# Products of no use behind each flag product, behind the list counts and ahead of the first turned rows of the first routing

## The chip, the cores and the metric

The kernel runs on one core of one Trainium2 chip. The metric is the device time of one execution in microseconds (us), the median of several runs. TensorE is called PE, VectorE DVE, ScalarE ACT, GpSimd POOL and SyncE SP.

## What is computed

Three layers follow each other. A gated linear attention over 768 steps makes 3072 rows of 320 numbers. A mixture of eight experts gives each row to one expert, 384 rows to each, in the order of all gate logits; the rows of an expert then go through that expert's two matrices. A dense layer with an exponential unit ends it.

```python
def _moe_ref(x, w_gate, w1, w2):
    logits = x @ w_gate
    order = np.argsort(-logits.flatten())
    for idx in order:                       # greedy, largest logit first
        tok, e = (int(idx) // E, int(idx) % E)
        if assigned[tok] >= 0 or counts[e] >= cap:
            continue
        assigned[tok] = e
        counts[e] += 1
    for e in range(E):
        mask = assigned == e
        h = np.maximum(x[mask] @ w1[e], 0.0)
        out[mask] = h @ w2[e]

def _moe2_ref(x, w_in, w_out):
    h = x @ w_in
    g = np.where(h > 0.0, h, np.exp(np.minimum(h, 0.0)) - 1.0)
    return g @ w_out
```

## The kernel before, in words

The attention runs first, in 24 units. Then comes the routing, in eight rounds: each round finds the one expert whose list fills next, and the 384 rows of that list. The first round must be done before any expert work can start; rounds 1 to 7 are recorded in between the matmuls of the expert and dense layers (the class `Mlp`). Each engine works through its own list of instructions in the order in which they were recorded.

**The first round** (`Router.round` with `r == 0`) looks for a threshold on the logits in six steps, some bits at a time. A step after the first is a circle of two engines:

- DVE subtracts the last digit (`j`, L831; `d`, L834) and builds a table of comparisons (`ge`, L630).
- PE counts with it, in 12 small matmuls into `pr` (L802; the first step has 24 at L817).
- DVE compares the counts with what each expert can still take and writes flags (`half` L669, `flag` L670; `fl` L820 in the first step).
- PE sums the flags over the partitions in one matmul of 8 columns (L828, **the flag product**), and DVE reduces its result to the next `j`.

In between, one piece of the conversion of the last weight matrix (`wout_pieces`) is recorded in each step. It uses DVE (`wt`, L967 and L974), POOL (the product `wt<-wt,wx` at L977 and the subtraction `wol` at L1082) and ACT.

After the sixth step DVE finds the expert (`m`) and the rows of its first weights (`wi`, L845). POOL gathers the expert's first matrix with `wi` (`stg`, L1104). PE makes **the list counts**, three matmuls (`p1`, L863 to L865). DVE numbers the members of the list with them, and PE turns the numbers into row indices in 24 small matmuls (L889). DVE adds these up to `idx`, and POOL gathers with it the 384 rows in three pieces (`xg`), and behind them the expert's second matrix (`stg<-in_w2a`).

**The first turned rows** are made in `prep_x(0)`: for each of the three pieces PE transposes (L1176), ACT and DVE split the result into two parts (`xh` L1193, `xl` L1184). Then PE starts on the expert's first product (P1, `ph` at L1223) and goes on with the second (C1, `acc` at L1315 and after).

**Products of no use.** `spin(n)` (L1158) records n matmuls of 512 columns with the dense layer's weights `wih`, whose result `junk` nobody reads. `prep_x(0)` has them ahead of each piece's transposes and behind the last: `WARM = [8, 2, 2, 2]`. `junk` is one of the three PSUM buffers `acc`. The attention has such a row too, at its start (L145).

Of the kernel before, what the change touches and what calls it, by code (L numbers as in the profile page):

```python
# [8 lines left out]
F32 = mybir.dt.float32  # L9
# [21 lines left out]
SPIN, MX = 12, [256, 512, 640]  # L31
TG = 20
NB, NL, PX = 2, 3, 0.2
WARM = [8, 2, 2, 2]


class Plan:
# [50 lines left out]
    def next(self):  # L88
        self.due(min(self.todo)[0])
# [462 lines left out]
class Router:  # L552
# [180 lines left out]
    def round(self, r):  # L733
# [21 lines left out]
        if last:  # L755
            te = self.T([128, 8], F32, "te")
            V.scalar_tensor_tensor(te, neg, 0.0, self.w8, op0=ALU.is_equal, op1=ALU.mult)
            plan.dve(170)
        else:
            steps = STEPS[r > 0]  # L760
            if r > 0:
                Lm = self.T([128, 8, 24], F32, "Lm")
                V.scalar_tensor_tensor(Lm, neg[:, :, None].to_broadcast([128, 8, 24]), 3e38, L, op0=ALU.mult, op1=ALU.add)
                V.scalar_tensor_tensor(rem, neg, -3e38, rem, op0=ALU.mult, op1=ALU.max)
                V.tensor_reduce(b, Lm.rearrange("p i c -> p c i"), AX, ALU.max)
                yield plan.dve(1130) - HOP, "d", 0
                dg = self.digits(r)
                next(dg)
                V.tensor_tensor(self.cols(Lm), self.cols(Lm), self.over(b, 8), op=ALU.is_equal)
                next(dg)  # L770
                V.tensor_tensor(self.cols(Lm), self.cols(Lm), self.values(1, 8), op=ALU.mult)
                next(dg, 0)
                d = self.T([128, 24, 2], BF, "d")
                V.tensor_copy(d, self.D[:, 0, :, None].to_broadcast([128, 24, 2]))
                V.tensor_reduce(a8, Lm.rearrange("p i c -> p c i"), AX, ALU.max)
                yield plan.dve(2370) - HOP, "d", 0
                V.scalar_tensor_tensor(a8, ax, 0.0, a8, op0=ALU.is_equal, op1=ALU.mult)
                self.low_digits(r)
                plan.dve(1320)
                V.tensor_tensor(self.cols(A), self.values(1, 8), self.over(a8, 8), op=ALU.is_equal)  # L780
                plan.dve(350)
            for i in range(len(steps)):
                end = i == len(steps) - 1
                if i or r:
                    ge = self.pairs(d, ALU.is_ge)
                    self.table = self.made
                    t = plan.dve(600)
                    if i == 1 and r == 0:
                        self.low_digits(r)
                    if end:  # L790
                        d1 = self.T([128, 24], F32, "d1")
                        V.tensor_scalar(d1, d[:, :, 0], 1.0, None, op0=ALU.add)
                    else:
                        h = self.T([128, 24], F32, "h")
                        V.scalar_tensor_tensor(h, d[:, :, 0], 64.0, self.Df[:, i + 1], op0=ALU.mult, op1=ALU.add)
                    plan.dve(176)
                    yield t, "", 400
                    pk = self.psum()
                    fl = self.flag[i % 2]
                    if r == 0:  # L800
                        for g in range(12):
                            PE.matmul(pk[:64, :16].rearrange("p (i b) -> p i b", b=2), ge[:, g * 64:g * 64 + 64],  # L802
                                      A[:, :, g * 2:g * 2 + 2], start=g == 0, stop=g == 11)
                        yield plan.small(320), "d", 0
                        self.halves(pk[:64, :16].rearrange("p (i b) -> p b i", b=2), rem, fl[:32])
                    for g in range(6 if r else 0):
                        PE.matmul(pk[:, :32].rearrange("p (i b) -> p i b", b=4), ge[:, g * 128:g * 128 + 128],  # L807
                                  A[:, :, g * 4:g * 4 + 4], start=g == 0, stop=g == 5)
                    if r:
                        yield plan.small(160), "d", 0  # L810
                        self.fold(pk[:, :32].rearrange("p (i b) -> p b i", b=4), rem, fl[:32], ALU.is_ge)
                    t = plan.dve(793 if r else 320)
                else:
                    fl = self.T([128, 8], BF, "fl")
                    pk = self.psum()
                    for c in range(24):
                        PE.matmul(pk[:, :8], self.g0[:, c], A[:, :, c], start=c == 0, stop=c == 23)  # L817
                    yield plan.small(624), "d", 0
                    next(self.dg)
                    V.tensor_tensor(fl, pk[:, :8], rem, op=ALU.is_ge)  # L820
                    for _ in self.dg:
                        pass
                    h = self.T([128, 24], F32, "h")
                    V.scalar_tensor_tensor(h, self.Df[:, 0], 64.0, self.Df[:, 1], op0=ALU.mult, op1=ALU.add)
                    t = plan.dve(540)
                yield t, "", 400 if i else 0
                pn = self.psum()[:, :8]
                PE.matmul(pn, self.ones if end else self.onz, fl, start=True, stop=True)  # L828
                yield plan.small(39), "d", 0
                j = self.T([128, 1], F32, "j")  # L830
                V.tensor_reduce(j, pn, AX, ALU.max)  # L831
                if not end:
                    d = self.T([128, 24, 2], BF, "d")
                    V.tensor_scalar(d, h[:, :, None].to_broadcast([128, 24, 2]), j, None, op0=ALU.subtract)  # L834
                    plan.dve(440)
            te = self.T([128, 8], F32, "te")
            V.scalar_tensor_tensor(te, pn, j, self.w8, op0=ALU.is_equal, op1=ALU.mult)
# [25 lines left out]
        PE.matmul(p1[:, :48], self.ones, mm, start=True, stop=True)  # L863
        PE.matmul(p1[:, 48:], self.tri, mm, start=True, stop=False)
        PE.matmul(p1[:, 48:], self.far, mm, start=False, stop=True)  # L865
        yield plan.small(90), "d", 0
        inc = self.T([128, 48], F32, "inc")
        iv = self.T([128, 24], I32, "iv")
# [40 lines left out]
class Mlp:  # L909
# [255 lines left out]
    def prep_x(self, r):  # L1165
# [6 lines left out]
        def turn(k):  # L1172
            for t in range(3):
                if (r, t) == (0, 0):
                    self.twice(k, 0)
                nc.tensor.transpose(ps[k][0][:, t * 128:t * 128 + 128], self.xg[k][:, t * 128:t * 128 + 128], self.ident)  # L1176
# [20 lines left out]
        if r == 0:  # L1197
            ps = [self.psum() for t in range(3)]
            for k in range(3):
                self.spin(WARM[k])  # L1200
                turn(k)
                split(k)
            self.spin(WARM[3])
            return
# [283 lines left out]
    def start(self, first):  # L1488

        nc = self.nc  # L1490
        fill = self.fill
        self.ws = {}
        early = []
        need = "d"
        for k, (_, _, gap) in enumerate(first):
            if gap and k > FK:
                self.after(self.router.table)
                while True:
                    d = "d" in need
                    _, need = next(fill)  # L1500
                    if d and "d" in need:
                        break
            if not early and 0 in self.router.res:
                for i in range(3):
                    self.get_w(0, i)
                early = [q for i in range(3) for q in self.pieces(i)]
        self.routed = 0
        self.get_x(0)
        self.after()
        for h, l, x, p in early:  # L1510
            nc.scalar.activation(h, x, AF.Copy)
        for k, (h, l, x, p) in enumerate(early):
            nc.vector.tensor_tensor(l[p], x[p], h[p], op=ALU.subtract)
            if k % 2 and k < 4:
                self.get_w(0, 3 + k // 2)
        self.wsplit = 3
        routes = self.routes(1)
        for _ in range(R1):
            next(routes)
        plan = self.plan  # L1520
        plan.reset()
        self.junk = self.acc.tile([128, 512], F32, name="acc")
        for _ in self.prep_x(0):
            pass
        return fill, routes
# [137 lines left out]
```

## Time and profile before

| | before |
|---|---|
| median of 3 runs | 754.86 us (754.59 to 755.6) |
| the profiled execution's own time | 750.71 us |
| its span, first to last instruction | 748.9 us |
| its mean granted TensorE clock | 0.969 of 2.4 GHz |
| PE busy | 702.9 us (94%) |

The profiled execution is 4.15 us shorter than the median of the runs. Everything read from the trace is on the profile's own clock; what a change adds or takes away there is added to the median.

### The profile page before, as it was taken

The page shows a single profiled execution, that of the slowest core. Times are in us where ns is not written, and L with a number is a line of the kernel's source. Part 1 is how long each engine was busy: PE and PEld are TensorE (multiplying, and loading weights), DVE is VectorE, ACT ScalarE, POOL GpSimd, SP SyncE. Part 2 cuts the span into 40 slices and gives each one's busy share as a digit, 9 for nine tenths or more (in the row PEclk, how much of TensorE's full clock was granted, in tenths as well). Part 3 has the DMA queues.
Part 4 walks back from the last instruction along what each step waited for, and adds up shares of the span by engine and source line. Part 5 has one row for each costly group of instructions (what it writes and reads, how often), then busy time and mean ns, then how long its engine had stood idle before and what let it go on. Part 6 is the DMA issues. An engine that isn't in the chain of part 4 may idle for free.

```text
span 748.9 us, 17930 instructions
## 1 busy us (share of the span) xinstructions
PE 702.9 (94%) x7274; PEld 639.3 (85%) x7274; DVE 541.3 (72%) x1592; ACT 377.6 (50%) x804; POOL 186.6 (25%) x242
## 2 busy tenths in 40 slices
PE   7889888837999999999999999999999999999997
PEld 4656666626989999999999999999999999999997
DVE  8687888887898968965896698569868833851442
ACT  5455445435365725842772366256527743752443
POOL 5666655235111401210301120112022220001001
PEclk9899999957999999999999999999999999999999
DMA  7777968236002301400320230022013321100000
GB/s 280 237 231 226 251 212 261 51 109 214 18 1 85 124 1 51 131 28 1 103 80 28 85 93 5 27 85 98 1 30 109 112 88 45 36 1 26 1 2 27
DMA packets 22436, 67.31 MB, mean 90 GB/s; under 512 B 3536, under 2 KB 7632, under 8 KB 22352
## 3 DMA queue, kind: packets, MB, share of 16 engines
q1 hardware_dynamic: 14240, 35.12, 15.4%
q0 software_dynamic: 8064, 30.94, 12.4%
q8 instruction: 57, 0.93, 0.5%
q14 instruction: 27, 0.22, 0.1%
q10 hardware_dynamic: 48, 0.10, 0.0%
HBM read 58.28 MB, written 7.86 MB: 88 GB/s over the span
## 4 chain that ended last, share of the span: by engine, by line
PE 73%; issue 11%; DVE 9%; ACT 3%; POOL 2%; DMA 1%; POOLq 0%; SPq 0%; ACTq 0%; DVEq 0%
PE ph L1223 30%; PE acc L1362 6%; PE acc L1366 6%; PE acc L1363 6%; PE acc L1330 3%; PE acc L1332 3%; PE acc L1331 2%; PE pO L381 2%; PE pR L395 2%; PE pX L464 2%; PE acc L1317 1%; PE acc L1319 1%; PE pX L450 1%; PE pr L807 1%; PE pO L365 1%
## 5 line engine op out<-in xcount | busy, mean ns | idle before, releaser
L1276 DVE SCALAR_TENSOR_TENSOR e<-e,ph 128x384 f32<-128x384 f32 x128 | 70.3, 550 | 50.4 <-ACT e L1273 49.7
L1272 ACT ACTIVATE e<-ph 128x384 f32<-128x384 f32 x128 | 62.5, 488 | 79.4 <-PE ph L1223 74.3
L1223 PE MATMUL ph<-yh,wih 128*128 128x384 f32 x256 | 89.1, 348 | 0.7 <-DVE xl L1184 0.4
L1240 ACT ACTIVATE gh<-ph 128x384 fp32r<-128x384 f32 x64 | 31.3, 491 | 114.0 <-PE ph L1223 89.1
L1223 PE MATMUL ph<-yh,wil 128*128 128x384 f32 x256 | 86.1, 337 | 0.0
L1375 POOL DMA_INDIRECT out_dram<-ot,idx x24 | 24.0, 998 | 210.8 <-ACT ot L1093 207.8
L1100 DVE TENSOR_TENSOR gl<-e,gh 128x384 fp32r<-128x384 f32 x128 | 70.9, 561 | 1.8 <-ACT gh L1093 0.3
L1273 ACT ACTIVATE e<-e 128x384 f32<-128x384 f32 x128 | 67.3, 526 | 4.0
L1362 PE MATMUL acc<-woh,gh 128*128 128x320 f32 x216 | 68.3, 316 | 0.0
L1247 DVE SCALAR_TENSOR_TENSOR gl<-ph,gh 128x384 fp32r<-128x384 f32 x64 | 35.2, 552 | 45.5 <-ACT gh L1240 45.3
L1366 PE MATMUL acc<-woh,gl 128*128 128x320 f32 x216 | 66.9, 310 | 0.5 <-DVE gl L1100 0.5
L1363 PE MATMUL acc<-wol,gh 128*128 128x320 f32 x216 | 66.8, 309 | 0.0
L1223 PE MATMUL ph<-yl,wih 128*128 128x384 f32 x256 | 66.0, 338 | 0.0
L1093 ACT ACTIVATE gh<-e 128x384 fp32r<-128x384 f32 x96 | 49.0, 514 | 11.4 <-DVE e L1276 11.1
L1366 PE MATMUL acc<-woa,gl 128*128 128x320 f32 x168 | 52.4, 312 | 0.9 <-DVE gl L1100 0.9
L1362 PE MATMUL acc<-woa,gh 128*128 128x320 f32 x168 | 52.8, 314 | 0.0
L1223 PEld LDWEIGHTS ph<-yh,wih 128*128 128x128 f32 x256 | 48.1, 188 | 4.8 <-ACT yh L1335 4.1
L1363 PE MATMUL acc<-wob,gh 128*128 128x320 f32 x168 | 51.8, 308 | 0.0
L1223 PEld LDWEIGHTS ph<-yh,wil 128*128 128x128 f32 x256 | 48.1, 188 | 0.0
L1104 POOL DMA_INDIRECT stg<-in_w1a_dram,wi x16 | 15.7, 983 | 123.3 <-DVE wi L845 119.0
L1223 PEld LDWEIGHTS ph<-yl,wih 128*128 128x128 f32 x256 | 46.1, 188 | 0.0
L1223 PE MATMUL ph<-xh,w1h 128*128 128x384 f32 x128 | 44.6, 349 | 0.1
(290 smaller groups left out, 2041.4 us busy)
## 6 DMA issues: line engine op xcount, KB each, us to landing
vk<-in_vk_dram SPq DMA_DIRECT2D x24, 484.0 KB, 5.4
qk<-in_qk_dram SPq DMA_DIRECT2D x20, 320.0 KB, 5.5
cx<-in_win_dram SPq DMA_DIRECT2D x8, 512.0 KB, 5.1
xd<-x SPq DMA_DIRECT2D x48, 80.0 KB, 3.4
wx<-in_wout_dram SPq DMA_DIRECT2D x9, 320.0 KB, 3.0
cx<-in_wout_dram SPq DMA_DIRECT2D x5, 448.0 KB, 4.1
qk<-in_qk_dram SPq DMA_DIRECT2D x4, 512.0 KB, 6.1
cx<-in_win_dram SPq DMA_DIRECT2D x4, 256.0 KB, 5.7
```

Of the source, the lines that this page charges most:

```text
L1093: self.nc.scalar.activation(out, x, AF.Copy)
L1100: self.nc.vector.tensor_tensor(out, x, y, op=ALU.subtract)
L1223: PE.matmul(p, w, x, start=k == 0, stop=k == 7)
L1240: nc.scalar.activation(h, p, AF.Relu)
L1247: nc.vector.scalar_tensor_tensor(l, p, 0.0, h, op0=ALU.max, op1=ALU.subtract)
L1272: nc.scalar.activation(e, p, AF.Relu, scale=-1.0)
L1273: nc.scalar.activation(e, e, AF.Exp, scale=-1.0)
L1276: nc.vector.scalar_tensor_tensor(e, e, -1.0, p, op0=ALU.add, op1=ALU.max)
L1362: PE.matmul(p, h[:, c], wh, start=f == 0, stop=False)
L1363: PE.matmul(p, h[:, c], wl, start=False, stop=False)
L1366: PE.matmul(p, l[:, c], wh, start=False, stop=f == 15)
L1375: s = nc.gpsimd.indirect_dma_start(out=self.out, out_offset=bass.IndirectOffsetOnAxis(ap=idx[:, t:t + 1], axis=0), in_=o, in_offset=None)
```

## The change

Three things are done, all in the first routing round and the turn behind it. Five products of no use follow each of the six flag products. Eight follow the list counts. Ahead of the first transposes stand twelve in place of eight. For this the buffer `junk` is allocated earlier, and the router is given the function `spin`.

```diff
-WARM = [8, 2, 2, 2]
+WARM = [12, 2, 2, 2]
...
                 pn = self.psum()[:, :8]
                 PE.matmul(pn, self.ones if end else self.onz, fl, start=True, stop=True)
+                if r == 0:
+                    self.idle(5)
                 yield plan.small(39), "d", 0
...
         PE.matmul(p1[:, 48:], self.far, mm, start=False, stop=True)
+        if r == 0:
+            self.idle(8)
         yield plan.small(90), "d", 0
...
         nc = self.nc
         fill = self.fill
+        self.junk = self.acc.tile([128, 512], F32, name="acc")
+        self.router.idle = self.spin
...
         plan.reset()
-        self.junk = self.acc.tile([128, 512], F32, name="acc")
         for _ in self.prep_x(0):
```

On PE, at the second of the six flag products, the list changes as follows (`onz` and `flag` are the operands of the flag product, `ge` and `A` those of the next counts):

```order
 L828 LDWEIGHTS onz
 L828 MATMUL pr<-flag_319,onz 128x8
+L1162 MATMUL acc<-wih 128x512 x5
 L802 LDWEIGHTS ge
 L802 MATMUL pr<-A,ge 64x16
```

The counts of the next step now stand behind five products of 512 columns. It is the same at the other flag products; DVE, ACT, POOL and SP have the same instructions in the same order as before.

On PE, from the last flag product to the row indices, before (`mm` marks the list's members):

```order
L828 LDWEIGHTS ones
L828 MATMUL pr<-flag_319,ones 128x8
L863 LDWEIGHTS ones
L863 MATMUL pr<-mm,ones 128x48
L864 LDWEIGHTS tri
L864 MATMUL pr<-mm,tri 128x48
L865 LDWEIGHTS far
L865 MATMUL pr<-mm,far 128x48
L889 LDWEIGHTS ge
L889 MATMUL pr<-R,ge 64x24
```

The same place now (the lines below the first insertion have moved by two, those below the second by four):

```order
L828 LDWEIGHTS ones
L828 MATMUL pr<-flag_319,ones 128x8
L1162 MATMUL acc<-wih 128x512 x5
L865 LDWEIGHTS ones
L865 MATMUL pr<-mm,ones 128x48
L866 LDWEIGHTS tri
L866 MATMUL pr<-mm,tri 128x48
L867 LDWEIGHTS far
L867 MATMUL pr<-mm,far 128x48
L1162 MATMUL acc<-wih 128x512 x8
L893 LDWEIGHTS ge
L893 MATMUL pr<-R,ge 64x24
```

Five products now stand between the last flag product and the list counts, and eight between these and the 24 matmuls of the row indices.

## Rows read from the trace of the kernel before

**Rows 1.** The page: the granted clock in 40 slices of 18.7 us.
```profile
PEclk9899999957999999999999999999999999999999
```

**Rows 2.** Windows around the first routing; PEclk is the share of 2.4 GHz.
```profile
146.00:149.50 3.50, 1.85 (x13) 1.45 (x13) 3.16 (x15) 1.17 (x3) 0.72 (x1) 1.00 0.23 55
150.00:153.00 3.00, 1.41 (x27) 1.15 (x27) 2.08 (x16) 1.01 (x3) 0.00 (x0) 0.50 0.95 317
...
168.00:173.00 5.00, 1.69 (x28) 1.65 (x27) 3.08 (x14) 1.23 (x3) 3.03 (x3) 0.50 0.59 175
173.00:176.50 3.50, 3.50 (x8) 2.40 (x8) 2.50 (x10) 1.91 (x4) 1.96 (x2) 0.50 0.94 326
177.00:181.50 4.50, 3.44 (x16) 1.92 (x17) 4.12 (x7) 3.04 (x8) 3.95 (x4) 1.00 0.42 98
```

**Rows 3.** Windows in the attention, around the first fall of the clock.
```profile
26.00:27.70 1.70, 0.00 (x0) 0.00 (x0) 0.82 (x2) 1.67 (x3) 0.42 (x1) 1.00 0.63 183
...
30.50:33.50 3.00, 2.58 (x66) 2.03 (x67) 1.71 (x3) 1.36 (x4) 3.00 (x4) 0.50 0.58 166
33.50:36.50 3.00, 3.00 (x66) 2.16 (x69) 0.51 (x1) 0.00 (x0) 0.68 (x1) 0.50 0.84 237
```

**Rows 4.** Timeline of PE in the routing: start, length, instruction, idle before and releaser.
```profile
152.25 0.17 PE L828 MATMUL pr<-fl,onz 128*128 128x8 bf16 x1 [0.26 <-DVE fl L820]
153.81 0.81 PE L802 MATMUL pr<-A,ge 128*64 128x16 bf16 x12 [1.39 <-DVE ge L630]
...
156.38 0.81 PE L802 MATMUL pr<-A,ge 128*64 128x16 bf16 x12 [1.13 <-DVE ge L630]
...
159.00 0.81 PE L802 MATMUL pr<-A,ge 128*64 128x16 bf16 x12 [1.19 <-DVE ge L630]
...
162.18 0.81 PE L802 MATMUL pr<-A,ge 128*64 128x16 bf16 x12 [1.73 <-DVE ge L630]
...
168.68 0.20 PE L863 MATMUL pr<-mm,ones 128*128 128x48 bf16 x1 [1.89 <-DVE mm L857]
...
168.75 0.21 PE L865 MATMUL pr<-mm,far 128*128 128x48 bf16 x1
171.58 1.41 PE L889 MATMUL pr<-R,ge 128*64 128x24 bf16 x24 [2.62 <-DVE R L882]
172.92 3.78 PE L1158 MATMUL acc<-wih 128*128 128x512 f32 x8
177.40 0.44 PE L1176 MATMUL ph<-ident,xg 128*128 128x128 f32 x2 [0.70 <-DMA xg<-xd,idx]
```

**Rows 5.** Timelines of DVE and POOL: the conversion's pieces in three steps.
```profile
154.93 0.30 DVE L967 TENSOR_SCALAR wt<-wx 128x320 int32<-128x320 int32 x1
...
157.50 0.50 DVE L967 TENSOR_SCALAR wt<-wx 128x320 int32<-128x320 int32 x1
...
160.20 0.98 DVE L967 TENSOR_SCALAR wt<-wx 128x320 int32<-128x320 int32 x1
...
156.95 0.87 POOL L977 TENSOR_TENSOR wt<-wt,wx 128x320 f32<-128x320 f32 x1 [9.31 <-DVE wt L974]
...
160.12 0.87 POOL L977 TENSOR_TENSOR wt<-wt,wx 128x320 f32<-128x320 f32 x1
```

**Rows 6.** From the row indices to C1: timeline of POOL, chain of waits, timeline of PE.
```profile
174.13 0.95 POOL L1104 DMA_INDIRECT xg<-xd,idx  x1 [1.44 <-DVE inc L904]
...
178.97 4.80 DMA stg<-in_w2a_dram,wi
...
188.25 0.44 PE L1315 MATMUL acc<-gh,w 128*128 128x384 f32 x1 [0.88 <-DVE w L1100]
```

**Rows 7.** Lengths: timeline of PE at the start, and two pieces of the chain.
```profile
1.21 5.21 PE L145 MATMUL pF<-wz 128*128 128x512 bf16 x12 [1.21 <-DVE warm L149]
...
189.91 2.77 PE ph L1223 x16
...
199.18 0.16 PE pr L807 x6
```

## The prediction

> **What bounds the kernel now.** I read the page first. It shows where the granted TensorE clock sinks: the two lowest digits, 5 and 7, stand for 150 to 187 us, where the attention is over and the first routing runs [rows 1]. Windows over that place come next. The clock is at 2.4 GHz until 149.5 us, at 1.2 GHz from 150 on through the whole routing, and at 2.4 GHz again when PE turns the first rows; in between PE was busy less than half of 150 to 153 and a third of 168 to 173, and then all of 173 to 176.5, where the eight products of no use run, and behind them the clock is up [rows 2]. So the clock is low where PE has little to do. What is worth anything there is what each step waits for last, so I went on to the timeline of PE, where each count, list count and index matmul starts with the release by DVE [rows 4], to the timelines of DVE and POOL for what DVE itself waits for [rows 5], and to the chain of waits for what starts the expert work [rows 6].
>
> Three readings carry the rest.
>
> First, a step goes round between DVE and PE, and PE is idle 1.1 to 1.7 us between a flag product and the next counts [rows 4]. That idle is the room for the new products.
>
> Second, from the third step on PE is not what the circle waits for. DVE's L967 stands behind the flags in DVE's order and ahead of `j`. It took 0.30 us in the first step, where POOL was still, 0.50 us in the next and 0.98 in the one after, and these two times it ended 0.18 to 0.19 us after POOL's L977 did: 158.00 against 157.82, and 161.18 against 160.99 [rows 5]. So POOL's piece, which follows the table of the same step, fixes when `j` comes; flags that are earlier or somewhat later don't move it.
>
> Third, behind the indices POOL gathers the rows from 174.13 on, then the second matrix, whose transfer is the next piece of the chain; C1 starts at 188.25, and PE has then waited 0.88 us for that matrix [rows 6]. So a delay of the indices goes to the end in full, and a delay of P1 alone only from 0.88 us on. After that PE has little idle time, and I let the shift go through to the end.
>
> **The change part by part.** Price of one product: at 1.2 GHz 12 took 5.21 us, 0.434 each [rows 7]. At 2.4 GHz 16 matmuls of 384 columns took 2.77 us, 0.173 each [rows 7], so 512 columns are 0.23. Five are 2.17 us or 1.15 us, eight 3.47 or 1.85, twelve 5.2 or 2.8.
>
> Step 1. The first flag product starts at 152.25 and the next counts at 153.81 [rows 4]. The clock is at 1.2 GHz there [rows 2], and the products can't have lifted it before they ran. They end at about 152.30 + 2.17 = 154.47: **+0.66 us**. Bounds: 0, if this execution's clock had not yet sunk, and 0.66.
>
> Step 2. From the flag product to the counts at 156.38 are 1.13 + 0.19 = 1.32 us [rows 4]. At 2.4 GHz the products fit (1.15 + 0.05). At 1.2 GHz the counts are 0.90 late; L967 there is held by POOL, alone it takes 0.30 in place of 0.50 [rows 5], so 0.20 are covered and 0.70 stay. The clock may come up during these products: I take the middle, **+0.35**, bounds 0 and 0.70. Faster counts bring nothing here, since POOL holds L967.
>
> Steps 3 to 5. The idle is 1.19 us before the counts at 159.00 and 1.73 before those at 162.18 [rows 4], with the flag product 1.38 and 1.92. At 1.2 GHz the counts come 0.84 and 0.30 late. L967 takes 0.98 in the later steps where 0.30 would do [rows 5], so some 0.65 of lateness is covered there. **0**, bounds 0 and 0.20. For the same reason counts that take half their 0.81 us gain nothing.
>
> Behind the sixth flag product the idle is 1.89 + 0.19 = 2.08 us: at 1.2 GHz 0.14 late. Behind the list counts there are 171.58 - 168.75 = 2.83 us [rows 4] for eight products: 0.64 late at 1.2 GHz, not at all at 2.4. The thirteen products stand close together, so the clock may come up among them: **+0.20** for both, bounds 0 and 0.78.
>
> The row indices, 24 matmuls in 1.41 us at 1.2 GHz [rows 4], are on the path: DVE adds them up right behind. The nearest row at 2.4 GHz is a later round's six counts in 0.16 us, 0.027 each [rows 7]; 24 of them and a tail of 0.15 are 0.8. The gain is 0 to 0.6. Since the clock is likelier up than not behind thirteen products: **-0.40**.
>
> The twelve before the turned rows. The first rows land at 177.40, 4.5 us after the eight products begin at 172.92 [rows 4]. Twelve at 2.4 GHz are over after 2.8 us; at 1.2 GHz they would take 5.2 and end 0.7 late, which the 0.88 us before C1 cover. **0** for the delay. But at 2.4 GHz PE then stands idle for some 1.6 us. In the attention PE stood idle for 1.7 us up to 27.7; the clock was still up then, but low by 30.5 and stayed so to 36.5, though PE was busy 2.58 of the first 3.00 us and all of the next [rows 3]. So P1 may begin at 1.2 GHz, where it began at 2.4 in the profiled execution. Ahead of C1 stand four of its eight pieces, 32 matmuls, 5.5 us at 2.4 GHz [rows 7]. 3 us at the low clock lose 1.5, less the 0.88: +0.6; 6 us, as in rows 3, lose 3.0, less 0.88: +2.1. I take **0**, since the runs of before need not have had the good clock that the profiled one had, and keep 0 to +2.1.
>
> Moving `junk` costs nothing: the buffer is free from the attention's last read, and its order on the other engines is unchanged.
>
> Sum: 0.66 + 0.35 + 0 + 0.20 - 0.40 + 0 = **+0.8 us** on the profiled 750.71, so 751.5 there, and 754.86 + 0.8 = **755.7 us** for the median.
>
> A rule that speaks on this: the Trainium skill, page "TensorE: Matmul & The Clock Gate", section "A second HAM failure mode: psum-queue depth-cycling", says that short idles between groups of matmuls can send the clock up and down again, and that the throughput goes lost in these changes. By that rule the time would be that of the second rival below. The traces so far agree as far as the fall behind an idle of 1.7 us goes [rows 3]; no row shows bursts of five.
>
> **The rivals.** A measurement of this kernel can tell about 0.2%, 1.5 us, from no change.
>
> *The clock stays at 1.2 GHz until the row indices (slower).* For it: the clock stayed low through 30.5 to 33.5 with PE nearly always busy [rows 3], and the routing keeps a hole behind each count, while DVE makes the flags. Against it: after eight products in a row the clock was up [rows 2]. Price: 0.66 + 0.70 + 0.20 + 0.14 + 0.64 and no gain: **+2.3 us, 757.2**. It decides from the second flag product on: if the counts of step 2 start about 2.2 us after it, this is the case.
>
> *The clock goes up and falls again, and P1 begins low.* At 2.4 GHz a step of 3.2 us holds 1.15 + 0.5 us of PE work, half of it, and the idle before the turned rows is 1.6 us. Then the sum above holds, and P1 costs 0.6 more: **+1.4 us, 756.3**; with the index matmuls at 1.2 GHz too +1.8. The page of the Trainium skill named above speaks for this one.
>
> *The clock is up from the start (faster).* If the clock had not yet sunk at the first flag product, the products keep it: step 1 costs 0, its counts take 0.5 in place of 0.81 us (-0.3), the indices gain 0.6: **-0.9 us, 754.0**. If runs of before also start P1 at 1.2 GHz (3 us of it, 0.6 beyond its cover) and the changed kernel doesn't, **-1.5 us, 753.3**. Against it: the profiled clock was low by 150, 2.2 us before that product [rows 2, 4]. For it: the runs are 4.15 us above the profiled execution, and something in them is slower that the trace doesn't show.
>
> **How the numbers follow.** Forecast, +0.8 us: 0.50. Low clock throughout: 0.17. Up and down with a low P1: 0.15. Clock up from the start: 0.18. The first lies within 0.2%; of the second nearly all is slower, of the third half, of the fourth some two thirds are beyond -0.2%. That makes faster 0.12, same 0.63, slower 0.25. The predicted time is 755.7. The range goes down to -1.8 us (the clock up, and P1 gaining 0.9, nearer to the 0.6 of the one bound than to the 2.1 of the other) and up to +2.9 (the low clock throughout, 2.3, with a P1 of 0.6): 753.1 to 757.8. The likeliest case alone has 754.9 to 756.4.
>
> **What would show it.** Right: the counts after the first flag product start some 2.2 us behind it; later steps keep their 3.2 us; L967 still ends 0.2 us after L977; the granted clock is 1.00 in part of 156 to 170; the index matmuls take 0.8 to 1.0 us; C1 starts 0 to 1.5 us later than 188.25. Wrong: the clock at 0.50 through all steps; or P1's matmuls 0.34 us apart; or a C1 that starts earlier; or the steps 3 to 5 shorter than 3.1 us, which would say that PE was in their circle after all.

## The result and the profile after

The changed kernel takes 758.58 us in the median of 15 runs (756.86 to 764.42), beside 754.86 us (751.36 to 756.69 in 15 runs) before. The ratio is 1.0064, with a 95% interval from 1.0044 to 1.0083: slower, by 3.3 to 6.3 us. The forecast was 755.7 and no change; the time lies above the range.

The profiled execution took 757.82 us with a span of 756.0, 7.1 more than that of before. The timeline of PE shows how much of this is the change. Columns: start, length, instruction, idle before it and what ended it.

```profile
154.64 0.17 PE L828 MATMUL pr<-fl,onz 128*128 128x8 bf16 x1 [0.26 <-DVE fl L820]
154.67 2.48 PE L1162 MATMUL acc<-wih 128*128 128x512 f32 x5
157.08 0.81 PE L802 MATMUL pr<-A,ge 128*64 128x16 bf16 x12
158.33 0.19 PE L828 MATMUL pr<-flag,onz 128*128 128x8 bf16 x1 [0.44 <-DVE flag L670]
158.38 2.48 PE L1162 MATMUL acc<-wih 128*128 128x512 f32 x5
160.79 0.81 PE L802 MATMUL pr<-A,ge 128*64 128x16 bf16 x12
162.04 0.19 PE L828 MATMUL pr<-flag,onz 128*128 128x8 bf16 x1 [0.44 <-DVE flag L670]
...
164.49 0.81 PE L802 MATMUL pr<-A,ge 128*64 128x16 bf16 x12
...
173.16 0.19 PE L828 MATMUL pr<-flag,ones 128*128 128x8 bf16 x1 [0.44 <-DVE flag L670]
...
175.49 0.26 PE L865 MATMUL pr<-mm,ones 128*128 128x48 bf16 x1
...
175.62 0.21 PE L867 MATMUL pr<-mm,far 128*128 128x48 bf16 x1
175.66 3.76 PE L1162 MATMUL acc<-wih 128*128 128x512 f32 x8
179.35 0.93 PE L893 MATMUL pr<-R,ge 128*64 128x24 bf16 x24
180.21 3.01 PE L1162 MATMUL acc<-wih 128*128 128x512 f32 x12
184.44 0.62 PE L1180 MATMUL ph<-ident,xg 128*128 128x128 f32 x3 [1.23 <-DMA xg<-xd,idx]
...
195.43 0.34 PE L1319 MATMUL acc<-gh,w 128*128 128x384 f32 x1
```

The first flag product stands at 154.64, 2.39 us later than before [rows 4], ahead of the first added product. The instructions up to there are the same; in the profiled executions below, those that leave this part as it is reach the first flag product between 150.98 and 158.69. That spread is the attention's and not the change's. It is why stretches are compared here that begin at the first flag product.

From there to C1 it is 195.43 - 154.64 = 40.79 us, before 188.25 - 152.25 = 36.00 [rows 4, 6]: **+4.79 us**, inside the 3.3 to 6.3 us of the ratio. Behind C1 nothing is added or won back: from there to the end it is 560.57 us, before 560.65. In place of an idle that DVE ends, the counts now stand without an idle behind the five products, and these end 2.4 us after the flag product. By places, in us (before by rows 4, an idle and the flag product's 0.19 added up):

| from, to | before | after | measured | forecast |
|---|---|---|---|---|
| flag product 1, counts | 1.56 | 2.44 | +0.88 | +0.66 |
| flag product 2, counts | 1.32 | 2.46 | +1.14 | +0.35 |
| flag product 3, counts | 1.38 | 2.45 | +1.07 | 0 |
| flag products 4 and 5, counts | 1.92 each | 2.47, 2.45 | +1.08 together | 0 |
| flag product 6, list counts | 2.08 | 2.33 | +0.25 | +0.20 with the next |
| list counts, row indices | 2.83 | 3.73 | +0.90 | |
| row indices, length | 1.41 | 0.93 | -0.48 | -0.40 |

The windows of the changed kernel answer to those of before [rows 2]; the column behind POOL's is the clock as a share of 2.4 GHz, the second is PE's busy time.

```profile
158.00:163.00 5.00, 4.23 (x21) 3.09 (x22) 3.15 (x14) 1.34 (x3) 0.88 (x1) 0.50 0.14 31
163.00:168.00 5.00, 4.56 (x22) 2.90 (x20) 2.83 (x11) 1.35 (x3) 2.75 (x3) 0.50 0.33 103
168.00:173.00 5.00, 4.28 (x31) 2.95 (x30) 2.23 (x10) 1.56 (x4) 2.96 (x4) 0.50 0.24 66
173.00:176.50 3.50, 3.34 (x11) 2.44 (x12) 2.15 (x12) 1.14 (x3) 1.17 (x2) 0.50 0.34 96
177.00:181.50 4.50, 4.50 (x36) 3.23 (x35) 2.15 (x11) 1.69 (x3) 1.52 (x3) 0.75 0.77 267
```

PE is now busy for 4.2 to 4.6 of 5 us and still has 1.2 GHz in every one of the six steps. Only at the end of the eight products behind the list counts does the clock come up: a window from 175.6 to 179.3 has 0.50, one from 179.3 to 182 has 1.00.

POOL and DVE, in the third step of the changed kernel, show what became of POOL's hold on L967 (now L971; POOL's L977 is now L981):

```profile
160.23 0.88 POOL L981 TENSOR_TENSOR wt<-wt,wx 128x320 f32<-128x320 f32 x1 [10.19 <-DVE wt L978]
...
161.63 0.16 DVE L669 SCALAR_TENSOR_TENSOR half<-pr,rem 32x8 f32<-32x8 f32 x1 [1.54 <-PE pr L802]
161.83 0.15 DVE L670 TENSOR_TENSOR flag<-pr,half 32x8 bf16<-32x8 f32 x1
161.91 0.30 DVE L971 TENSOR_SCALAR wt<-wx 128x320 int32<-128x320 int32 x1
```

L971 takes 0.30 us, since POOL is through with its piece, at 161.11, before the flags are there. So the hold is gone, 0.2 to 0.7 us a step, and nobody has it back: DVE has the next table ready earlier, and waits 1.54 us for counts that stand behind the five products.

### The profile page after: what moved, and what is told of

Read it like the earlier page. It is cut to its first block, busy times and chain, and to the rows that moved or that the text cites. A ratio compares the mean times of both kernels' runs of the same rounds, so it can differ in the third digit from the quotient of the medians.

```text
span 756.0 us, 18011 instructions
## 1 busy us (share of the span) xinstructions
PE 717.8 (95%) x7313; PEld 650.7 (86%) x7316; DVE 539.5 (71%) x1592; ACT 377.9 (50%) x804; POOL 184.6 (24%) x242
## 4 chain that ended last, share of the span: by engine, by line
PE 77%; issue 10%; DVE 7%; ACT 2%; DMA 2%; POOL 1%; POOLq 0%; SPq 0%; ACTq 0%; DVEq 0%
PE ph L1227 31%; PE acc L1366 6%; PE acc L1370 6%; PE acc L1367 6%; PE acc L1334 3%; PE acc L1162 3%; PE acc L1336 2%; PE acc L1335 2%; PE pO L381 2%; PE pR L395 2%; PE pX L464 2%; PE acc L1321 1%; PE acc L1323 1%; PE pX L450 1%; DMA vk<-in_vk_dram 1%
## 5 line engine op out<-in xcount | busy, mean ns | idle before, releaser
L1251 DVE SCALAR_TENSOR_TENSOR gl<-ph,gh 128x384 fp32r<-128x384 f32 x64 | 35.2, 553 | 45.4 <-ACT gh L1244 45.2
L1227 PE MATMUL ph<-yh,wis 128*128 128x384 f32 x128 | 44.7, 349 | 0.0
```

The costliest lines, as they stand in the source:

```text
L1227: PE.matmul(p, w, x, start=k == 0, stop=k == 7)
L1251: nc.vector.scalar_tensor_tensor(l, p, 0.0, h, op0=ALU.max, op1=ALU.subtract)
```

## The experiments

Each kernel was timed on the same chip as the kernel before (four chips in all), and the stretch from the first flag product to C1 was read from one execution of each (36.00 us before, 40.79 changed). Single executions differ in it: from the start of the row indices to C1, where a_flags, d_two, e_fill, f_fit, h_narrow and k_ten have nothing changed, they take 16.48 to 16.97 us, before 16.67. So a few tenths of a us to C1 are no finding by themselves. The earlier place of the buffer is in every run, and d_two, g_list5 and h_narrow show no loss with it.

| run | what it has | ratio (95%) | to C1, us |
|---|---|---|---|
| a_flags | five behind each flag product | 1.0060 (1.0036 to 1.0084) | 40.27 |
| b_list | eight behind the list counts | 1.0014 (0.9991 to 1.0037) | 36.19 |
| c_warm | twelve ahead of the turned rows | 1.0024 (0.9996 to 1.0053) | 35.94 |
| d_two | two behind each flag product | 1.0005 (0.9978 to 1.0032) | 36.31 |
| e_fill | five, and two behind the counts | 1.0048 (1.0022 to 1.0075) | 38.50 |
| f_fit | three, and one behind the counts | 1.0025 (1.0006 to 1.0044) | 36.76 |
| g_list5 | five behind the list counts | 0.9996 (0.9970 to 1.0022) | 36.19 |
| h_narrow | five of 256 columns | 0.9984 (0.9958 to 1.0011) | 36.27 |
| i_early | the change, and products in the attention's end | 1.0016 (0.9987 to 1.0045) | 42.01 |
| j_both | that, and two behind the counts | 0.9988 (0.9962 to 1.0013) | 36.37 |
| k_ten | ten behind each flag product | 1.0055 (1.0027 to 1.0082) | 40.64 |
| l_hold | j_both, and the wait for the rows filled | 1.0024 (0.9999 to 1.0050) | 36.42 |

**a_flags, b_list, c_warm: the three parts alone.** Each keeps one of the three edits; the buffer's earlier place is in all.

```diff
 a_flags: -WARM = [12, 2, 2, 2]   +WARM = [8, 2, 2, 2]   -self.idle(8)
 b_list:  -WARM = [12, 2, 2, 2]   +WARM = [8, 2, 2, 2]   -self.idle(5)
 c_warm:  -self.idle(5)           -self.idle(8)
```

> The change with only the five products behind each flag product; none behind the list counts, eight ahead of the turned rows as before. Theory 1 (the products run at 1.2 GHz and each group of five takes 2.45 us, longer than the idle it stands in): the counts start 2.4 to 2.5 us behind every flag product, the six places together cost 0.88 + 1.13 + 1.07 + 0.54 + 0.54 + 0.25 = 4.4 us, ratio 1.0058. Theory 2 (the loss comes from the clock at the turned rows and P1, moved by the other products): within 1 us of the kernel before.

> The change with only the eight products behind the list counts. Theory 1: they take about 3.7 us at 1.2 GHz in an idle of 2.83, so the row indices start 0.9 us late; the index matmuls take 0.9 to 1.4 us as the clock is up or not; together +0.4 to +0.9 us, ratio 1.0005 to 1.0012. Theory 2: +2 us or more, with P1 at 1.2 GHz.

> The change with only the twelve products ahead of the first turned rows. Theory 1: the first rows land 4.4 us behind the row indices and twelve products at 1.2 GHz take 5.4, so PE turns them up to 1 us late, which the wait of C1 for the second matrix covers: 0 to +0.3 us. Theory 2: +2 us or more.

The five products alone give nearly the whole loss, +4.3 of 4.8 us to C1 and a ratio of 1.0060. The other two edits alone give +0.2 and -0.1 us to C1, and ratios whose intervals hold 1. Theory 1 stands; theory 2, by which the loss came from the clock at the turned rows, falls: a_flags loses as much with those products as they were. In b_list the row indices start 0.6 us late but take 0.93 us, so the two nearly cancel.

**d_two and h_narrow: products that fit.** d_two has two products in place of five; h_narrow has five that are half as wide.

```diff
-                    self.idle(5)
+                    self.idle(2)
...
+            self.nc.tensor.matmul(self.junk[:, :256], self.wih[:, 0, :128], self.wih[:, 0, :256], start=True, stop=True)
```

> Two products behind each flag product in place of five, and neither of the other two edits. Theory 1: two take about 1.0 us at 1.2 GHz, less than the shortest idle of 1.3, so nothing is late and the clock stays at 1.2 GHz: 0 us. Rival (any product in the circle delays it, by the load of its weights or of the counts' behind it): +0.2 us in each of five steps, +1 us.

> Only the flag products' part, with products of 256 columns in place of 512. Theory 1 (the columns set the price): five take 1.1 to 1.4 us at 1.2 GHz, about the idle of the second step: +0 to +0.4 us on the kernel before, 36.0 to 36.4 us from the first flag product to C1. Rival (loading the same weights anew for each product sets it): five still take 1.7 us or more, +1 us and more.

Timeline of PE in h_narrow, second step:

```profile
157.40 0.19 PE L828 MATMUL pr<-flag,onz 128*128 128x8 bf16 x1 [0.44 <-DVE flag L670]
157.44 1.41 PE L1167 MATMUL acc<-wih 128*128 128x256 f32 x5
158.79 0.81 PE L802 MATMUL pr<-A,ge 128*64 128x16 bf16 x12
```

The counts follow 158.79 - 157.40 = 1.39 us behind the flag product, beside 1.32 before. The row indices start 19.34 (d_two) and 19.37 us (h_narrow) behind the first flag product, before 19.33; the 0.3 us more to C1 arise behind them, and neither time can be told from that of before. With a shorter group the loss goes. The rivals (every product delays; the load of the weights sets the price) fall: five of 512 columns take 2.41 us to the next counts and five of 256 take 1.35, so 256 columns are worth 0.21 each, and 0.29 us a group is left that does not depend on the columns.

**e_fill and f_fit: no hole behind the counts.** One or two products more stand behind each later count, where PE waits for the flags; f_fit has three in place of five behind the flag product.

```diff
+                        self.idle(2)
                         yield plan.small(320), "d", 0
                         self.halves(pk[:64, :16]...
```

> Only the flag products' part of the change, and two products more behind each of the five later counts, where PE otherwise waits 0.44 us for the flags. Theory 1 (the bursts of five left the clock low because of the hole behind the counts): with the hole filled PE runs without a break and the clock is up from the second or third step on; from there five products take 1.2 us, a step takes again 2.6 to 3.2 us, and from the first flag product to C1 it is 37 to 38.5 us, where the kernel before has 36.0 and the five alone 40.3: +1 to +2.5 us on the kernel before. Rival (no burst of this kind lifts the clock in these steps): each of five steps grows by another 0.5 us, 42.5 to 43 us from the first flag product to C1, +6.5 to +7 us.

> Three products behind each flag product and one behind each later count; eight ahead of the turned rows, none behind the list counts. Theory 1: three take about 1.45 us at 1.2 GHz and one 0.45 to 0.5, so steps 1 and 2 are late by about 0.2 each and the others not: 36.0 to 36.8 us from the first flag product to C1, and at most 36 if the clock comes up, since POOL's pieces set the later steps: -0.3 to +0.8 us on the kernel before. Rival (every product costs its length): 4 products of 0.48 us in five steps, +3 us and more.

Windows of e_fill, over the first two steps and over the later ones:

```profile
151.00:157.50 6.50, 6.50 (x26) 4.25 (x25) 4.08 (x21) 0.00 (x0) 0.38 (x1) 0.50 0.00 0
158.50:171.50 13.00, 9.49 (x71) 6.15 (x71) 10.89 (x39) 4.90 (x11) 6.86 (x7) 1.00 0.35 103
```

Timeline of PE in e_fill, the later steps:

```profile
158.93 0.18 PE L829 MATMUL pr<-flag,onz 128*128 128x8 bf16 x1
158.97 1.41 PE L1163 MATMUL acc<-wih 128*128 128x512 f32 x5
160.31 0.55 PE L802 MATMUL pr<-A,ge 128*64 128x16 bf16 x12
...
161.35 0.18 PE L829 MATMUL pr<-flag,onz 128*128 128x8 bf16 x1
...
164.51 0.18 PE L829 MATMUL pr<-flag,onz 128*128 128x8 bf16 x1
...
167.71 0.18 PE L829 MATMUL pr<-flag,ones 128*128 128x8 bf16 x1
```

Timelines of POOL and DVE in e_fill, at the fourth flag product (L972 is the L967 of before):

```profile
160.35 1.08 POOL L1087 TENSOR_TENSOR wol<-wt,woh 128x320 fp32r<-128x320 f32 x1 [2.35 <-DVE h L795]
161.39 0.88 POOL L982 TENSOR_TENSOR wt<-wt,wx 128x320 f32<-128x320 f32 x1
...
161.46 0.99 DVE L972 TENSOR_SCALAR wt<-wx 128x320 int32<-128x320 int32 x1 [0.23 <-POOL wol L1087]
```

With seven products a step the clock is up from about 158.2 on. The five then take 1.34 us to the counts, and the last two steps take 164.51 - 161.35 = 3.16 and 3.20 us: no less than before at 1.2 GHz, where the counts took 0.81 us and not 0.55. The flags come earlier, but DVE then waits for POOL and its L972 ends 0.18 us after POOL's piece: POOL's pieces, not PE, set these steps. The step ahead of them is not so bound: it takes 161.35 - 158.93 = 2.42 us, before 2.63. What e_fill lost, 2.5 us, it lost in the first two steps. The traced execution is the fastest of its 11 (752.01 us beside a median of 757.88).

Windows of f_fit over its six steps:

```profile
156.00:161.00 5.00, 5.00 (x33) 3.17 (x31) 3.76 (x18) 0.00 (x0) 0.81 (x1) 0.50 0.00 0
161.00:166.00 5.00, 5.00 (x24) 2.94 (x24) 3.96 (x15) 2.69 (x6) 2.09 (x4) 0.50 0.32 82
166.00:172.00 6.00, 5.95 (x34) 3.83 (x34) 4.85 (x17) 2.37 (x7) 3.67 (x4) 0.50 0.34 100
```

Here PE is busy for 15.95 of 16 us and the clock stays at 1.2 GHz. So filling the hole behind the counts, which theory 1 took for the reason in e_fill, is not enough to bring the clock up; k_ten below brings it up with the hole left open, but with ten products. Whether e_fill needed the filled hole beside its seven products is not shown. The price of f_fit is that of theory 1, +0.76 us to C1, 0.54 of it ahead of the row indices.

**g_list5: five behind the list counts.** `self.idle(5)` in place of `self.idle(8)`, and nothing behind the flag products.

> Five products behind the list counts in place of eight, nothing else of the change but the earlier buffer. Theory 1: five take 2.4 us at 1.2 GHz, less than the idle of 2.83, so the row indices start on time; with the clock still low they take 1.41 us (0), with the clock up 0.9 (-0.5): 35.5 to 36.0 us from the first flag product to C1, ratio 0.9993 to 1.0. Rival (the clock falls again before the turned rows and P1 runs at 1.2 GHz): C1 without a wait for DVE, up to +1 us.

The row indices start on time, with an idle of 0.31 us ahead of them, and take 1.41 us at 1.2 GHz: nothing won and nothing lost (ratio 0.9996). The 0.19 us to C1 are within what single executions differ by.

**k_ten: twice as many.** `self.idle(10)` in place of `self.idle(5)`, without the other two edits.

> Ten products behind each flag product in place of five, neither of the other two edits. Theory 1: at 1.2 GHz they take 4.8 us, so a step grows to 6.1 us; if the clock stays low six groups cost 14 us more than five a group do; if ten a step lift it from the second or third step on, ten take 2.5 us and the later steps are 3.3 to 3.8 us: +3 to +7 us on the kernel before, no worse than five a step although there are twice as many. Rival (the price is the number of products alone): +18 us.

Timeline of PE in k_ten, second and third step:

```profile
158.16 0.18 PE L828 MATMUL pr<-flag,onz 128*128 128x8 bf16 x1 [0.44 <-DVE flag L670]
158.20 2.54 PE L1162 MATMUL acc<-wih 128*128 128x512 f32 x10
160.67 0.55 PE L802 MATMUL pr<-A,ge 128*64 128x16 bf16 x12
161.65 0.18 PE L828 MATMUL pr<-flag,onz 128*128 128x8 bf16 x1 [0.44 <-DVE flag L670]
```

The clock is up from 157 to 176, ten products take 2.5 us at 2.4 GHz, as five do at 1.2, and the loss is the same (40.64 and 40.27 us to C1). What is lost is length beyond the idle, at either clock.

**i_early, j_both, l_hold: a clock that is up from the start.** The whole change, with products in the idle of the attention's last units:

```diff
+                self.keep(2)
                 self.logits(u - 1)
...
+        self.keep(1)
         self.turn(u)
+        self.keep(2)
         self.logits(u)
+        self.keep(3)
         hook(NU)
```

`keep` makes bf16 products of 512 columns into `pF`. j_both adds e_fill's two behind the counts, l_hold also `WARM = [19, 4, 4, 2]`.

> The whole change, and products of no use in the idle of the attention's last three units as well (two ahead of each of the last gate-logit groups, one ahead of the last turn, three behind the last group). Theory 1 (the products cost what they do because the clock is at 1.2 GHz when they run): if the clock is still up at the first flag product, the first five take 1.4 us and fit; whether five a step then hold it up is open: 35 to 36.5 us from the first flag product to C1 if they do, 38 to 41 if it falls in the steps. Rival (the products cost more than their idle at either level): 39 us and more although the clock is up.

> As the run before it, with two more products behind each later count. Theory 1: with the clock up from the start seven products a step hold it, as they did from the second step on where the holes were filled: later steps of 2.4 to 3.2 us as POOL's pieces allow, row indices in 0.9 us, 35 to 35.8 us from the first flag product to C1, -0.3 to -1 us on the kernel before. Rival: the clock falls in spite of it, 38 us and more.

> As the last but one (products in the attention's last units, five behind each flag product and two behind each later count, eight behind the list counts), and the wait for the gathered rows filled as well: 19, 4, 4 and 2 products in place of 12, 2, 2 and 2. Theory 1: the clock stays up until P1 begins and through it; the row indices gain 0.5 to 0.6 us, P1 loses nothing, C1 starts 35.2 to 35.6 us behind the first flag product with a wait for DVE ahead of it: -0.4 to -0.8 us on the kernel before, ratio 0.9990 to 0.9995, too little to tell from none in the time. Rival (the low clock in the routing costs what it costs in a matmul-bound stage, half of some 25 us): 28 us, -8 us or more.

In i_early the clock was still up at the first flag product and fell at about 155.8, among the first five. The later steps then cost what they cost in the changed kernel, and P1 too began at 1.2 GHz: 42.01 us, more than the 38 to 41 expected. That execution is not typical of its kernel: 760.95 us at a mean clock of 0.969, beside a median of 756.51 and up to 0.988 in the other runs, and the ratio of 1.0016 does not show such a loss. So the trace shows what a fall of the clock costs here, not what i_early does as a rule. In j_both the clock was up through the steps, but had a mean of 0.83 in 176 to 186, where the rows are turned; C1 stands at 36.37 us where 35 to 35.8 was expected. In l_hold the clock stayed up. Windows of l_hold, from the attention's end to C1:

```profile
146.00:150.00 4.00, 3.79 (x73) 3.11 (x69) 3.51 (x11) 1.02 (x3) 0.75 (x1) 1.00 0.18 45
156.00:176.00 20.00, 16.61 (x132) 11.10 (x131) 16.77 (x65) 6.90 (x15) 8.86 (x10) 1.00 0.34 105
176.00:186.00 10.00, 8.68 (x55) 6.53 (x52) 7.00 (x15) 5.18 (x12) 7.25 (x7) 1.00 0.60 199
186.00:192.00 6.00, 5.89 (x34) 5.54 (x33) 4.20 (x10) 3.85 (x10) 1.81 (x2) 1.00 0.71 257
```

Timeline of PE in l_hold, from the first flag product to C1:

```profile
156.34 0.17 PE L839 MATMUL pr<-fl,onz 128*128 128x8 bf16 x1 [0.26 <-DVE fl L831]
...
175.61 0.90 PE L904 MATMUL pr<-R,ge 128*64 128x24 bf16 x24 [0.64 <-DVE R L897]
...
192.76 0.44 PE L1330 MATMUL acc<-gh,w 128*128 128x384 f32 x1 [0.51 <-DVE w L1115]
```

Timeline of DVE in l_hold, behind the row indices:

```profile
177.38 0.16 DVE L677 COPY half<-pr 32x12 f32<-32x12 f32 x1 [1.82 <-PE pr L904]
```

With 2.4 GHz throughout, the row indices start 175.61 - 156.34 = 19.27 us behind the first flag product; before, at 1.2 GHz, it was 171.58 - 152.25 = 19.33 [rows 4]. With twice the clock, and with the products that hold it, the routing up to the indices is 0.06 us shorter: the second step takes 2.43 in place of 2.57 us, the last two 3.20 and 3.21 where they took 3.17 and 3.18, and the list counts follow the sixth flag product after 2.29 in place of 2.08 us. No run has the high clock without products, so what it is worth alone is not shown. The indices take 0.90 us in place of 1.41, but DVE begins to add them up only 0.87 us after the last one's recorded end (0.83 in j_both), so this gain isn't there either. Where products stood right ahead of them, as in b_list, or at 1.2 GHz as before, DVE began 0.04 us after it. Why, no run settles: the ends of matmuls are modelled in the trace. C1 stands at 36.42 us, not at the 35.2 to 35.6 expected, and the time is not lower (1.0024, 0.9999 to 1.0050). The rival of a matmul-bound routing falls by far.

## Why the prediction was wrong

**The step that failed** is "Steps 3 to 5": zero, bounds 0 and 0.20. They cost 1.07 + 1.08 = 2.15 us. The reading behind it was right for these steps: POOL's piece holds L967, and faster counts gain next to nothing (2.58, 3.20 and 3.21 us in l_hold, where they took 2.63, 3.17 and 3.18). It was carried too far in step 2, where they gained 0.14. The conclusion did not follow: the hold on L967 lies between a flag product and the next counts, in the same stretch as the five products, so it was already in the idle of 1.92 us that I compared the products with. Two waits in one stretch run beside each other; the longer one counts. I took the shorter one off once more, as 0.65 us of cover. The trace after shows the hold gone (L971 takes 0.30 us) and the counts late all the same, 2.45 to 2.47 us behind the flag product. At the forecast's own price of a product, 0.84 + 2 x 0.30 = 1.44 of the 2.15 us come from this. The 0.20 us of cover in step 2 was the same mistake.

**The clock** was the second. I took the middle between a clock that comes up during the second group and one that doesn't. It stayed low in all six steps (the changed kernel, a_flags) and came up with seven or ten a step (e_fill, k_ten). My first rival, the low clock throughout, is what happened; but it was priced at +2.3 us with the same cover in it, and measured 4.8. Without the cover, with 2.22 us a group, its price would have been 0.66 + 0.90 + 0.84 + 2 x 0.30 + 0.14 + 0.64 = 3.8 us, and the range would have had to reach beyond that.

**The price of a group** was the third. One product was priced at 0.434 us by the attention's row [rows 7]; the trace has no record of the clock that early, but 0.43 is what a product takes in the steps, at a granted 0.50. What was left out is what a group costs beside its products. Timeline of PE in d_two, second step:

```profile
158.65 1.20 PE L1162 MATMUL acc<-wih 128*128 128x512 f32 x2
```

Two products last 1.20 us here, five 2.48 in the changed kernel and eight 3.78 at 1.2 GHz before [rows 2, 4]: each three more add 1.28 to 1.30 us, 0.43 a product. The counts follow the start of five after 2.41 us, which is 0.26 more than 5 x 0.43; h_narrow's sums give 0.29, with half the columns. From a flag product to the counts it is 2.44 to 2.47 us where 2.22 was reckoned, over the first five groups 1.2 us more.

**The list counts** were late by 1.15 us in place of 0.20, beyond the upper bound of 0.78, as the clock was low there too. **The indices** came out as said, 0.93 us, -0.48 where -0.40 was said, but narrowly: the clock came up just ahead of them. b_list alone gives +0.2 to C1 where these terms add to -0.2. The second rival's low clock was there **at the turned rows**, ahead of P1: PE stood idle 1.23 us before the first of them, the clock was down from 186 to 189.5, and C1 starts without a wait for DVE. It cost little, as the cover of 0.88 us [rows 6] took it. C1 comes 16.08 us behind the start of the indices, where it was 16.67.

**The rule that I weighed.** The Trainium skill, page "TensorE: Matmul & The Clock Gate", section "A second HAM failure mode: psum-queue depth-cycling", says that short idles between groups of matmuls send the clock up and down. The six steps show no such cycling: the clock stays low in them (0.50 in four windows). The same page, section "Why this matters for your kernels", advises to keep TensorE busy without a break to get the high clock. f_fit doesn't agree: busy for 15.95 of 16 us, and 0.50 all through.

**The faster rival** had its condition in j_both and l_hold, a clock that is up from the start, and its -0.9 us did not come: counts at twice the clock shorten the second step a little, and hardly the later ones, which POOL and DVE set.

## What to carry to other kernels

Before work is put into an engine's idle to lift its clock, compare its length at the low clock with each idle, one by one: that is the clock at which it starts, and what sticks out is paid every time. A wait that lies in the same stretch as the new work gives no cover; cover is only what comes behind it. And ask first what the higher clock could shorten: here the chain goes through DVE and POOL, and the routing at twice the clock on PE, with the products that held it, was 0.06 us shorter.

## What was not expected of the hardware

PE without a break is not yet PE at 2.4 GHz: in f_fit it was busy for 15.95 of 16 us with four products and twelve small matmuls a step, and stayed at 1.2; in e_fill, with seven products a step, the clock came up, and in k_ten with ten.

A group of products of no use costs more than its products: at 1.2 GHz 0.26 to 0.29 us more until the counts behind it start, with 512 columns and with 256 (a product of 512 columns takes 0.43). What this is made of, no run shows.

The times spread from run to run, over 5 us before and 8 us in the changed kernel, and in the profiled executions the first flag product moves between 150.98 and 158.69 us. The attention's clock falls at other places each time; I didn't try to hold it.
